# The second batch's transform input is loaded and split a step sooner, and SyncE's loads, two transpositions and token stores get a tied order

## The chip, the cores and the metric

The kernel runs on one core of one Trainium2 chip. The metric is the device time of one execution in microseconds (us). The time before is 1211.8 us, the median of three runs (1211.37, 1211.8 and 1213.98). Every time below that is not one of these comes from one profiled execution of the kernel before.

## The reference

Eight batches of 4224 tokens with 192 numbers each go through two stages. The first is a causal 7-tap convolution along the tokens, one set of softmaxed taps for each of 8 groups of 24 channels. The second adds the real part of a two-dimensional Fourier transform, normalizes each token and puts it through an MLP with a residual:

```python
out = np.einsum('hk,bskhg->bshg', w, x_unf)      # convolution, x of the rest
X = np.fft.fft(np.fft.fft(x, axis=1), axis=2)
u = x + np.real(X)
un = (u - mean(u)) / np.sqrt(var(u) + 1e-06)
result = u + np.maximum(un @ w_ch1, 0.0) @ w_ch2  # 192 -> 768 -> 192
```

## The kernel before

One token of a batch goes through these stages. Values are kept as pairs of 16-bit halves (high and low) where matmuls need the precision.

- **Convolution.** `conv_unit` (L443) multiplies windows of tokens with a band matrix on TensorE (PE) into `pc`, ScalarE (ACT) brings `pc` to `xa`, and `store_rows` (L381) writes `xa` to the scratch rows `sc` of the batch in DRAM. A batch has six chunks. For batch 1 the stores are given out by SyncE (SP), for later batches by ACT.
- **Load and split.** `load_x` (L533) reads `sc` back in another layout, in eight pieces `xs_0` to `xs_7`, given out by SP; four buffers serve the eight. `split_x` (L584) makes of each piece the halves XH on ACT (L594) and XL on VectorE (DVE, L602). Its scale `s_x` comes from the norm of the whole batch.
- **Transform.** `stage_a` (L608) multiplies XH and XL into `pa` and splits the result to `yh` (ACT) and `yl` (DVE), in 16 units per batch. `stage_b` (L660) makes `pb` and from it `V`, in 8 units. `prep` (L745) makes `pq`, adds it to the token rows `u` (DVE, L787, five instructions), takes the statistics (L794, L795 on DVE) and normalizes on GpSimd (POOL) to `hl`.
- **MLP.** `transposes` (L851) has SP give out the transposition of `hl` to `kt` (three buffers). `mlp_hidden` (L869) makes one sixth of the hidden layer: five matmuls into `ph` (L884, two PSUM buffers), `hh` on ACT (L888) and `hlo` on DVE (L889); a buffer of `ph` is free when `hlo` is done. `mlp_out` (L893) makes `po` (L903 to L909) and adds it to `u` on DVE (L915). `store_out` (L923) has SP write `u` to the output.

A batch has nine tiles of tokens, so the main loop (L1127) runs over 72 steps; step n has the hidden layer of tile n and the output layer of tile n−1. Steps 0 to 8 are those of batch 0, step 9 is the first of batch 1. Beside them, the front stages of later batches (convolution to `stage_b`) are strewn over the steps: `front` (L971) picks from tables by `rel`, the step minus the batch's first step. Batch 1 has tables of its own, `conv_1`, `load_1`, `split_1` and `a_1` (L963 to L966), since its front begins in the start-up; for it rel −9 is step 0.

Names: the profile writes `xs`, `kt` and so on without numbers. In the text `ph_3_4` is sixth 4 of step 3, `hlo_3_2` the low half of sixth 2 of step 3, `XH_1` and `XL_1` the halves made of `xs_1`, and `kt_2` the transposition for step 2 of the batch.

Each engine runs its instructions in the order in which a scheduler has put them, and a DMA is given out by the engine in whose order it stands. The scheduler goes by the order in which the program issues them and by its own costs; `tc.issue_after(x)`, also written `after(x)`, puts an instruction behind x. `in_turn()` puts XH behind the latest `hh` that was written before it. `turn[0]` is the latest transposition.

Of the kernel before, what the change touches and what calls it, by code (L numbers as in the profile page):

```python
# [35 lines left out]
AC = 32  # L36
# [93 lines left out]
def kernel(  # L130
# [250 lines left out]
    def store_rows(bt, xa, r0, cols):  # L381

        nw = xa.shape[1]
        full = min(nw, (S - r0) // WR)
        queue = nc.scalar if bt.b > 1 else nc.sync
        again = min(nw, max(0, (DUP - r0) // WR))
        for base, n in ((r0, full), (r0 + S, again)):
            if n:
                with after(turn[0] if bt.b == 1 else None):
                    store = queue.dma_start(  # L390
                        bt.sc[base : base + n * WR, cols].rearrange(
                            "(w p) d -> p w d", p=WR
                        ),
                        xa[:, :n],
                    )
        if full < nw:
            with after(turn[0] if bt.b == 1 else None):
              store = queue.dma_start(
                bt.sc[r0 + full * WR : S, cols], xa[: S % WR, full]
            )  # L400
        return store.ins
# [41 lines left out]
    def conv_unit(bt, ch, part, xa_slot=("xa", 2), slot=("f", 4), home=None):  # L443
# [41 lines left out]
        if part == 2:  # L485
            cols = slice(0, xt.shape[2])
            if b == 1:
                squares(bt, xt, bt.evicted)
            bt.last_store = store_rows(bt, xa[:, :, cols], ch * WC * WR, cols)
            del bt.xt[ch], bt.xa[ch]  # L490

    def conv_segments(bt):

# [39 lines left out]
    def load_x(bt, i):  # L533
# [5 lines left out]
        for c0, c1, wrap in ((0, cut, 0), (cut, 4, S)):  # L539
            if c0 == c1:  # L540
                continue
            src = bass.AP(
                bt.sc.tensor,
                bt.sc.offset + (33 * AC * c0 + 128 * b0 - wrap) * D,
                [[33 * D, AC * (c1 - c0)], [128 * D, b1 - b0], [1, D]],
            )
            with tc.issue_after(turn[0]) if b == 1 else ExitStack():
                load = nc.sync.dma_start(xs[AC * c0 : AC * c1, : b1 - b0], src)
        bt.xs[i] = xs
        return load.ins  # L550

    def load_first_x(bt):

# [297 lines left out]
    def transposes(bt, it):  # L851
        hl = bt.hl[it]
        n = hl.shape[1]
        kt = sb.tile([128, n, 128], F16, tag="kt", name=f"kt_{bt.b}_{it}", bufs=3)
        turn[0] = nc.sync.dma_start_transpose(kt, hl.rearrange("p n d -> p (n d)")).ins
        bt.kt[it] = kt.rearrange("p (g i) t -> p i g t", i=3)


# [63 lines left out]

    def store_out(bt, it):  # L923
        u = bt.u.pop(it)
        if it == Q0:
            nc.sync.dma_start(out0[bt.b], u[:, 0])
        else:
            nc.sync.dma_start(out1[bt.b, it].rearrange("p (g d) -> p g d", g=4), u)


    class Batch:
        def __init__(self, b):
            self.b = b
            self.nsq = 0
            self.V, self.xr, self.hl, self.kt = {}, {}, {}, {}
            self.u, self.h, self.po, self.xs, self.xt = {}, {}, {}, {}, {}
            self.xa = {}
# [13 lines left out]
    def call(f, *a):  # L951
        return lambda: f(*a)
# [8 lines left out]


    conv_1 = {-9: [4, 5]}  # L963
    load_1 = {-8: [0, 1, 2, 3], -7: [4, 5, 6, 7]}
    split_1 = {-7: [0, 1, 2, 3], -6: [4, 5, 6, 7]}
    a_1 = {-5: range(16)}  # L966

    def pause():
        pass
# [157 lines left out]
    for n in range(len(steps) + 1):  # L1127
# [24 lines left out]
                at.setdefault(min(first + i * step, len(main) - 1), []).append(f)  # L1152

        if n > 1:
            place([call(store_out, *steps[n - 2])], 0, 1)
        if n + 2 < len(steps):
            place(rest(n + 2), 0, 1)
            place([call(transposes, *steps[n + 2])], 3, 1)
        if n + 3 < len(steps):
            place(sums(n + 3), 2, 2)  # L1160
        if n + 5 < len(steps):
# [2 lines left out]
        for i, unit in enumerate(main):  # L1164
            merged += [unit, *at.get(i, ())]
        spread(merged, *fills)
    store_out(*steps[-1])


# [56 lines left out]
```

## Time and profile before

| what | value |
|---|---|
| median of three runs | 1211.8 us |
| the profiled execution's own time | 1214.54 us |
| its span, first to last instruction | 1212.7 us |
| PE busy | 1155.2 us (95%) |
| DVE busy | 891.5 us (74%) |
| POOL busy | 810.6 us (67%) |
| ACT busy | 637.2 us (53%) |
| share of PE in the chain that ended last | 86% |

The profile names the engines PE, DVE, ACT, POOL and SP; PEld is PE's load of weights, and a q behind an engine's name is the engine giving out a DMA. Times count from the start of the span. A row of the view by time tells the start, the length, the engine, the line, the operation with destination and source, how many were merged into the row, and in brackets how long the engine stood idle before and what ended that. The ends of PE's rows are modelled, so one begins before the last is listed as ended. The granted clock is 1.00 where PE runs at its full 2.4 GHz and 0.50 where it runs at 1.2.

Some starts in this execution, by the first `ph` of the step: step 1 at 115.72 us, step 2 at 129.63, step 3 at 144.64, step 4 at 162.74, step 9 at 249.06, step 10 at 268.85.

### The profile page before, as it was taken

What the parts mean: (1) busy time and instruction counts of PE and PEld (TensorE: products, weight loads), DVE (VectorE), ACT (ScalarE), POOL (GpSimd) and SP (SyncE); (2) the same over time, 40 slices, a digit from 0 to 9 for tenths busy, and PEclk for the clock granted to TensorE, in tenths of its full rate; (3) what the DMA queues carried; (4) which work ended last, traced back from release to release, by engine and by line L of the source; (5) the groups of instructions that cost most, each with busy time, mean ns of one, the idle gap of its engine ahead of it and who ended that gap; (6) DMA issues with size and microseconds to landing.
All of it is one profiled execution on the core that took longest, in us unless ns stands there. A gap on an engine that the chain in (4) does not pass through costs nothing.

```text
span 1212.7 us, 31442 instructions
## 1 busy us (share of the span) xinstructions
PE 1155.2 (95%) x12736; PEld 913.9 (75%) x12736; DVE 891.5 (74%) x2124; ACT 637.2 (53%) x1020; POOL 810.6 (67%) x1104
## 2 busy tenths in 40 slices
PE   4279999989999999999999999999999999999998
PEld 4178768867878778787877878787787878787766
DVE  7657686787867977688777978679777887566543
ACT  5547566555655556655655655555555554333222
POOL 0217875399747897389954997479963899677940
PEclk9589999989999999999999999999999999999999
DMA  8945856366565647474663956556474643333221
GB/s 307 257 119 149 219 166 147 110 170 122 150 162 141 145 122 182 133 173 115 152 170 100 200 117 175 137 146 167 114 179 124 160 104 76 89 65 92 69 56 43
DMA packets 238370, 170.56 MB, mean 141 GB/s; under 512 B 119369, under 2 KB 221969, under 8 KB 238225
## 3 DMA queue, kind: packets, MB, share of 16 engines
q1 hardware_dynamic: 184744, 109.95, 37.3%
q10 hardware_dynamic: 46952, 45.24, 13.6%
q0 software_dynamic: 6528, 13.38, 4.4%
q8 instruction: 99, 1.62, 0.6%
q14 instruction: 47, 0.38, 0.1%
HBM read 83.82 MB, written 58.55 MB: 117 GB/s over the span
## 4 chain that ended last, share of the span: by engine, by line
PE 86%; DVE 5%; DMA 4%; ACT 2%; issue 2%; SPq 1%; ACTq 0%; another core or an unknown queue 0%; DVEq 0%
PE ph L884 33%; PE po L903 10%; PE po L909 10%; PE po L906 10%; PE pa L619 6%; PE pq L769 6%; PE pb L672 5%; PE pc L468 4%; PE pa L646 1%; DMA xs<-sc 1%; PE pc L473 1%; DMA xs_yl<-sc 1%; DMA XL<-in_w_dram 1%; ACT XH L594 1%; DVE hlo L889 1%
## 5 line engine op out<-in xcount | busy, mean ns | idle before, releaser
L884 PE MATMUL ph<-kt,W 128*128 128x512 f16 (+1 forms) x2160 | 497.7, 363 | 6.4 <-DVE hlo L889 6.3
L888 ACT ACTIVATE hh<-ph 128x512 f16<-128x512 f32 (+1 forms) x400 | 236.6, 593 | 354.7 <-PE ph L884 336.8
L909 PE MATMUL po<-W,hlo 128*128 128x192 f16 x1584 | 384.5, 246 | 0.0
L903 PE MATMUL po<-W,hh 128*128 128x192 f16 x1584 | 384.4, 246 | 0.1
L906 PE MATMUL po<-W,hh 128*128 128x192 f16 x1584 | 384.1, 246 | 0.0
L889 DVE SCALAR_TENSOR_TENSOR hlo<-ph,hh 128x512 f16<-128x512 f32 (+1 forms) x400 | 269.0, 676 | 117.6 <-ACT hh L888 114.6
L884 PEld LDWEIGHTS <-W 128*128 128x128 f16 x2160 | 192.4, 98 | 142.6 <-issue 9.4
L824 POOL TENSOR_SCALAR un<-u,mv,y 128x192 f32<-128x192 f32 x260 | 274.9, 1065 | 7.8
L718 POOL DMA_INDIRECT u<-sc,rows_sb x136 | 154.5, 1136 | 31.4 <-issue 30.8
L903 PEld LDWEIGHTS <-hh 128*128 128x128 f16 x1584 | 154.8, 98 | 24.0 <-issue 0.3
L906 PEld LDWEIGHTS <-hh 128*128 128x128 f16 x1584 | 154.7, 98 | 21.4 <-issue 0.5
L909 PEld LDWEIGHTS <-hlo 128*128 128x128 f16 x1584 | 154.8, 98 | 19.7 <-issue 0.3
L841 POOL TENSOR_TENSOR hl<-un,hl 128x512 f16<-128x512 f32 (+2 forms) x142 | 129.3, 932 | 5.6
L787 DVE SCALAR_TENSOR_TENSOR u<-pq,g,u 128x128 f32<-128x128 f32 (+1 forms) x328 | 102.9, 380 | 28.5 <-PE pq L769 24.5
L815 POOL TENSOR_SCALAR v<-mv 128x4 f32<-128x4 f32 (+1 forms) x71 | 20.1, 282 | 145.7 <-DVE mv L795 128.2
L602 DVE SCALAR_TENSOR_TENSOR XL<-xs,s_x,XH 128x768 f16<-128x768 f32 (+1 forms) x56 | 93.2, 1664 | 22.9 <-ACT XH L594 22.9
L915 DVE SCALAR_TENSOR_TENSOR u<-po,fo,u 128x384 f32<-128x384 f32 (+1 forms) x136 | 81.1, 597 | 27.0 <-PE po L909 26.9
L594 ACT ACTIVATE XH<-xs,s_x 128x768 f16<-128x768 f32 (+1 forms) x56 | 94.3, 1686 | 9.1 <-DMA xs<-sc 9.0
L769 PE MATMUL pq<-c_sb,V 128*128 128x130 f16 (+1 forms) x1440 | 96.8, 215 | 0.1
L627 ACT ACTIVATE yh<-pa 99x512 f16<-99x512 f32 x112 | 65.2, 594 | 47.2 <-PE pa L619 40.3
L769 PEld LDWEIGHTS <-V 128*128 128x128 f16 (+1 forms) x1440 | 82.2, 100 | 8.3 <-issue 2.2
L619 PE MATMUL pa<-c_sb,XH 128*128 128x128 f16 x896 | 86.5, 219 | 0.0
(158 smaller groups left out, 1740.3 us busy)
## 6 DMA issues: line engine op xcount, KB each, us to landing
out_dram<-u SPq DMA_DIRECT2D x64, 384.0 KB
xt<-in_xw_dram ACTq DMA_DIRECT2D x30, 576.0 KB
sc<-xa ACTq DMA_DIRECT2D x30, 540.0 KB
xs<-sc SPq DMA_DIRECT2D x28, 288.0 KB
u<-sc SPq DMA_DIRECT2D x72, 96.0 KB
xt<-in_xw_dram SPq DMA_DIRECT2D x10, 576.0 KB
sc<-xa SPq DMA_DIRECT2D x10, 540.0 KB
xs<-sc SPq DMA_DIRECT2D x28, 192.0 KB
```

The costliest lines, as they stand in the source:

```text
L594: split = nc.scalar.activation(part(XH), src, AF.Copy, scale=bt.c)
L619: nc.tensor.matmul(pa[:, i], x[:, at], F[:, l], start=(n == 0), stop=(n == 2))
L718: nc.gpsimd.indirect_dma_start(to, None, bt.sc[:S], bass.IndirectOffsetOnAxis(ap=rows_sb[:, col : col + 1], axis=0),)
L769: mm = nc.tensor.matmul(po, weights(v, ND * r + k3), rhs[:, 0] if it == Q0 else rhs, start=(r + n == 0), stop=(r == 1 and n == 2),)
L824: (nc.vector if b + it == 0 else nc.gpsimd).tensor_scalar(un[:, g], u[:, g], mv[:, g, 0:1], y[:, g : g + 1], op0=ALU.subtract, op1=ALU.mult,)
L841: lower = (nc.vector if b + it == 0 else nc.gpsimd).tensor_tensor(bl[:, :, o : o + n], un[:, :ng, f], hi[:, :, f], op=ALU.subtract)
L884: nc.tensor.matmul(ph[:, n], W1[:, w, ht * 128 : (ht + 1) * 128], kt[:, k], start=(i == 0), stop=(i == len(order) - 1),)
L888: anchor[0] = nc.scalar.activation(hh, ph, AF.Relu).ins
L889: nc.vector.scalar_tensor_tensor(hlo, ph, 0.0, hh, op0=ALU.max, op1=ALU.subtract)
L903: nc.tensor.matmul(po[:, g % 2], hh[:, ht, tk], W2[:, ht, 0], start=(ht == 0), stop=False)
L906: nc.tensor.matmul(po[:, g % 2], hh[:, ht, tk], W2[:, ht, 1], start=False, stop=False)
L909: nc.tensor.matmul(po[:, g % 2], hlo[:, ht, tk], W2[:, ht, 0], start=False, stop=(ht == 5),)
```

## The change

Four edits. The tables of batch 1 move its loads from steps 1 and 2 to steps 0 and 1, its splits from steps 2 and 3 to steps 1 and 2, and the first eight of its sixteen `stage_a` units from step 4 to step 3. Its loads are no longer put behind the latest transposition, nor are the stores of its last two convolution chunks; the transpositions for steps 2 and 3 are put behind its last load that the program has issued by then. The store of a token tile is put behind the latest transposition, and stands in the program at the fifth place of its step where it stood at the first. In steps 0 and 1 the transposition for two steps later is issued at the end of the step.

```diff
--- before.py
+++ after.py
@@ -386,7 +386,7 @@
         again = min(nw, max(0, (DUP - r0) // WR))
         for base, n in ((r0, full), (r0 + S, again)):
             if n:
-                with after(turn[0] if bt.b == 1 else None):
+                with after(turn[0] if bt.b == 1 and not bt.ends else None):
                     store = queue.dma_start(
                         bt.sc[base : base + n * WR, cols].rearrange(
                             "(w p) d -> p w d", p=WR
@@ -394,7 +394,7 @@
                         xa[:, :n],
                     )
         if full < nw:
-            with after(turn[0] if bt.b == 1 else None):
+            with after(turn[0] if bt.b == 1 and not bt.ends else None):
               store = queue.dma_start(
                 bt.sc[r0 + full * WR : S, cols], xa[: S % WR, full]
             )
@@ -488,6 +488,7 @@
                 squares(bt, xt, bt.evicted)
             bt.last_store = store_rows(bt, xa[:, :, cols], ch * WC * WR, cols)
             del bt.xt[ch], bt.xa[ch]
+            bt.ends = ch > 2
 
     def conv_segments(bt):
 
@@ -544,10 +545,9 @@
                 bt.sc.offset + (33 * AC * c0 + 128 * b0 - wrap) * D,
                 [[33 * D, AC * (c1 - c0)], [128 * D, b1 - b0], [1, D]],
             )
-            with tc.issue_after(turn[0]) if b == 1 else ExitStack():
-                load = nc.sync.dma_start(xs[AC * c0 : AC * c1, : b1 - b0], src)
+            load = nc.sync.dma_start(xs[AC * c0 : AC * c1, : b1 - b0], src)
         bt.xs[i] = xs
-        return load.ins
+        bt.loaded = load.ins
 
     def load_first_x(bt):
 
@@ -852,7 +852,10 @@
         hl = bt.hl[it]
         n = hl.shape[1]
         kt = sb.tile([128, n, 128], F16, tag="kt", name=f"kt_{bt.b}_{it}", bufs=3)
-        turn[0] = nc.sync.dma_start_transpose(kt, hl.rearrange("p n d -> p (n d)")).ins
+        with after(batches[1].loaded if bt.b == 0 and it in (2, 3) else None):
+            turn[0] = nc.sync.dma_start_transpose(
+                kt, hl.rearrange("p n d -> p (n d)")
+            ).ins
         bt.kt[it] = kt.rearrange("p (g i) t -> p i g t", i=3)
 
 
@@ -922,16 +925,19 @@
 
     def store_out(bt, it):
         u = bt.u.pop(it)
-        if it == Q0:
-            nc.sync.dma_start(out0[bt.b], u[:, 0])
-        else:
-            nc.sync.dma_start(out1[bt.b, it].rearrange("p (g d) -> p g d", g=4), u)
+        with after(turn[0]):
+            if it == Q0:
+                nc.sync.dma_start(out0[bt.b], u[:, 0])
+            else:
+                nc.sync.dma_start(
+                    out1[bt.b, it].rearrange("p (g d) -> p g d", g=4), u
+                )
 
 
     class Batch:
         def __init__(self, b):
             self.b = b
-            self.nsq = 0
+            self.nsq, self.ends = 0, False
             self.V, self.xr, self.hl, self.kt = {}, {}, {}, {}
             self.u, self.h, self.po, self.xs, self.xt = {}, {}, {}, {}, {}
             self.xa = {}
@@ -961,9 +967,9 @@
 
 
     conv_1 = {-9: [4, 5]}
-    load_1 = {-8: [0, 1, 2, 3], -7: [4, 5, 6, 7]}
-    split_1 = {-7: [0, 1, 2, 3], -6: [4, 5, 6, 7]}
-    a_1 = {-5: range(16)}
+    load_1 = {-9: [0, 1, 2, 3], -8: [4, 5, 6, 7]}
+    split_1 = {-8: [0, 1, 2, 3], -7: [4, 5, 6, 7]}
+    a_1 = {-6: range(8), -5: range(8, 16)}
 
     def pause():
         pass
@@ -1152,10 +1158,11 @@
                 at.setdefault(min(first + i * step, len(main) - 1), []).append(f)
 
         if n > 1:
-            place([call(store_out, *steps[n - 2])], 0, 1)
+            place([call(store_out, *steps[n - 2])], 4, 1)
         if n + 2 < len(steps):
             place(rest(n + 2), 0, 1)
-            place([call(transposes, *steps[n + 2])], 3, 1)
+            if n > 1:
+                place([call(transposes, *steps[n + 2])], 3, 1)
         if n + 3 < len(steps):
             place(sums(n + 3), 2, 2)
         if n + 5 < len(steps):
@@ -1164,6 +1171,8 @@
         for i, unit in enumerate(main):
             merged += [unit, *at.get(i, ())]
         spread(merged, *fills)
+        if n < 2:
+            transposes(*steps[n + 2])
     store_out(*steps[-1])
```

What that does to the order on the engines, at three places.

The first place is in steps 0 to 2, on SP and on ACT. SP in steps 0 and 1: `sc` with `xa_5` are the last rows of batch 1, `xs` its loads, `kt` the transpositions for batch 0's steps, `u_0` the output of step 0. Before:

```order
L855 DMA_TRANSPOSE kt_2_1357<-hl_2_1299 128x12x128
L390 DMA sc_951<-xa_5_1392 120x5x192
L398 DMA sc_951<-xa_5_1392 24x192
L928 DMA out_dram<-u_0_622 128x768
L548 DMA xs_0_1543<-sc_951 128x4x192
L855 DMA_TRANSPOSE kt_3_1588<-hl_3_1529 128x12x128
L548 DMA xs_1_1599<-sc_951 128x5x192
```

Now, from the store of chunk 4 on:

```order
L390 DMA sc_951<-xa_4_1285 120x6x192
L856 DMA_TRANSPOSE kt_1_1109<-hl_1_1105 128x12x128
L390 DMA sc_951<-xa_5_1325 120x5x192
L398 DMA sc_951<-xa_5_1325 24x192
L548 DMA xs_0_1445<-sc_951 128x4x192
L548 DMA xs_1_1460<-sc_951 128x5x192
L548 DMA xs_2_1464<-sc_951 96x4x192
L548 DMA xs_2_1464<-sc_951 32x4x192
L548 DMA xs_3_1500<-sc_951 96x4x192
L548 DMA xs_3_1500<-sc_951 32x4x192
L548 DMA xs_4_1547<-sc_951 64x4x192 x2
L856 DMA_TRANSPOSE kt_2_1503<-hl_2_1304 128x12x128
```

The two stores stand ahead of kt_2 and not behind it; seven groups of loads follow them at once, with no transposition or output store between; kt_2 comes behind xs_4.

ACT in steps 1 and 2, where XH are the splits and `hh_1_2` is sixth 2 of step 1's hidden layer. Before:

```order
L231 ACTIVATE r_x_1485<-r_x_1485 128x1
L888 ACTIVATE hh_1_1495<-ph_1_2_1591 128x512
L888 ACTIVATE hh_1_1495<-ph_1_3_1628 128x512
L888 ACTIVATE hh_1_1495<-ph_1_4_1663 128x512
L681 ACTIVATE V_7_1688<-pb_7_0_1689 128x102x4
L888 ACTIVATE hh_1_1495<-ph_1_5_1680 128x512
L363 DMA xt_0_1723<-in_xw_dram 128x1152
L681 ACTIVATE V_7_1688<-pb_7_1_1704 128x102x4
L888 ACTIVATE hh_2_1725<-ph_2_0_1727 128x512
L888 ACTIVATE hh_2_1725<-ph_2_1_1771 128x512
L594 ACTIVATE XH<-xs_0_1543,s_x_1489 128x64x12
```

Now:

```order
L231 ACTIVATE r_x_1427<-r_x_1427 128x1
L681 ACTIVATE V_6_1468<-pb_6_0_1469 128x102x4
L681 ACTIVATE V_6_1468<-pb_6_1_1484 128x102x4
L594 ACTIVATE XH<-xs_0_1445,s_x_1431 128x64x12
L594 ACTIVATE XH<-xs_1_1460,s_x_1431 128x64x15
L891 ACTIVATE hh_1_1505<-ph_1_2_1604 128x512
L594 ACTIVATE XH<-xs_2_1464,s_x_1431 128x64x12
L891 ACTIVATE hh_1_1505<-ph_1_3_1644 128x512
L681 ACTIVATE V_7_1706<-pb_7_0_1707 128x102x4
L681 ACTIVATE V_7_1706<-pb_7_1_1722 128x102x4
```

XH_0 has moved from behind `hh_2_1` to the front of `hh_1_2`, with XH_1 next to it.

The second place is on DVE, at the end of step 2 and in step 3. Before, where XL_1 to XL_4 stand between the `hlo` of step 3:

```order
L889 SCALAR_TENSOR_TENSOR hlo_2_1726<-ph_2_5_1920,hh_2_1725 128x512
L602 SCALAR_TENSOR_TENSOR XL<-xs_1_1599,s_x_1489,XH 128x64x15
L889 SCALAR_TENSOR_TENSOR hlo_3_1934<-ph_3_0_1935,hh_3_1933 128x512
L415 TENSOR_SCALAR tot_0_1953<-nrm_1951 128x1
L602 SCALAR_TENSOR_TENSOR XL<-xs_2_1640,s_x_1489,XH 128x64x12
L915 SCALAR_TENSOR_TENSOR u_2_1111<-po_2_0_1967,fo,u_2_1111 128x384
L889 SCALAR_TENSOR_TENSOR hlo_3_1934<-ph_3_1_1996,hh_3_1933 128x512
L602 SCALAR_TENSOR_TENSOR XL<-xs_3_1720,s_x_1489,XH 128x64x12
L423 TENSOR_SCALAR wr_0_1957<-pn_0_1955 128x1
L602 SCALAR_TENSOR_TENSOR XL<-xs_4_1768,s_x_1489,XH 128x64x12
L787 SCALAR_TENSOR_TENSOR u_6_1533<-pq_6_2004,g_255,u_6_1533 128x192 x2
```

Now, the same stretch of `hlo`:

```order
L892 SCALAR_TENSOR_TENSOR hlo_2_1746<-ph_2_3_1878,hh_2_1745 128x512
L602 SCALAR_TENSOR_TENSOR XL<-xs_6_1656,s_x_1431,XH 128x64x12
L892 SCALAR_TENSOR_TENSOR hlo_2_1746<-ph_2_4_1912,hh_2_1745 128x512
L892 SCALAR_TENSOR_TENSOR hlo_2_1746<-ph_2_5_1929,hh_2_1745 128x512
L602 SCALAR_TENSOR_TENSOR XL<-xs_7_1738,s_x_1431,XH 128x64x12
L892 SCALAR_TENSOR_TENSOR hlo_3_1942<-ph_3_0_1943,hh_3_1941 128x512
L415 TENSOR_SCALAR tot_0_1996<-nrm_1994 128x1
L892 SCALAR_TENSOR_TENSOR hlo_3_1942<-ph_3_1_2031,hh_3_1941 128x512
```

Here the splits of xs_5 to xs_7 stand among step 2's `hlo`, and none stands behind `hlo_3_0`.

The third place is on ACT in step 7, where chunk 5 of batch 2's convolution is evicted to `xa_5` and stored. Before:

```order
L888 ACTIVATE hh_7_3340<-ph_7_2_3449 128x512
L888 ACTIVATE hh_7_3340<-ph_7_3_3486 128x512
L482 ACTIVATE xa_5_3249<-pc_5_0_3250,wg_5_3142 120x3x6x24
L482 ACTIVATE xa_5_3249<-pc_5_3_3270,wg_5_3142 120x3x6x24
L681 ACTIVATE V_2_3298<-pb_2_0_3299 128x102x4
L681 ACTIVATE V_2_3298<-pb_2_1_3314 128x102x4
L888 ACTIVATE hh_7_3340<-ph_7_4_3518 128x512
L482 ACTIVATE xa_5_3249<-pc_5_6_3330,wg_5_3142 120x2x6x24
L390 DMA sc_2047<-xa_5_3249 120x5x192
L398 DMA sc_2047<-xa_5_3249 24x192
L888 ACTIVATE hh_7_3340<-ph_7_5_3535 128x512
```

Now:

```order
L891 ACTIVATE hh_7_3340<-ph_7_0_3342 128x512
L891 ACTIVATE hh_7_3340<-ph_7_1_3380 128x512
L482 ACTIVATE xa_5_3249<-pc_5_0_3250,wg_5_3142 120x3x6x24
L482 ACTIVATE xa_5_3249<-pc_5_3_3270,wg_5_3142 120x3x6x24
L681 ACTIVATE V_2_3298<-pb_2_0_3299 128x102x4
L681 ACTIVATE V_2_3298<-pb_2_1_3314 128x102x4
L482 ACTIVATE xa_5_3249<-pc_5_6_3330,wg_5_3142 120x2x6x24
L891 ACTIVATE hh_7_3340<-ph_7_2_3448 128x512
L390 DMA sc_2101<-xa_5_3249 120x5x192
L398 DMA sc_2101<-xa_5_3249 24x192
L231 ACTIVATE r_x_3435<-r_x_3435 128x1
L891 ACTIVATE hh_7_3340<-ph_7_3_3486 128x512
```

The two stores stood behind `hh_7_4` and now stand behind `hh_7_2`.

## Rows read from the trace of the kernel before

**Rows 1.** The page, its first part (busy time of each engine, share of the span, instructions) and the first line of the chain that ended last, by engine.

```profile
PE 1155.2 (95%) x12736; PEld 913.9 (75%) x12736; DVE 891.5 (74%) x2124; ACT 637.2 (53%) x1020; POOL 810.6 (67%) x1104
...
PE 86%; DVE 5%; DMA 4%; ACT 2%; issue 2%; SPq 1%; ACTq 0%; another core or an unknown queue 0%; DVEq 0%
```

**Rows 2.** Who PE waited for from 110 us to the end of the span: engine, line and tile that waited, then what it waited for; total us, how often, the longest.

```profile
PE ph L884 <- DVE hlo L889: 6.3, 3, 3.4
PE pc L468 <- ACT xh L435: 1.9, 1, 1.9
```

**Rows 3.** Two stretches of 5 us: length, busy us of PE, PEld, DVE, ACT and POOL (each with its instructions), the granted clock, the DMA engines' share, GB/s.

```profile
155.00:160.00 5.00, 2.93 (x11) 1.51 (x11) 4.57 (x19) 0.60 (x2) 4.85 (x6) 0.71 0.48 150
255.00:260.00 5.00, 2.70 (x13) 1.30 (x13) 5.00 (x12) 0.81 (x2) 4.47 (x6) 0.61 0.65 188
```

**Rows 4.** Instructions of PE in order of time, steps 1 to 3: start, length, engine, line, operation, tile and operands, how many, and in brackets the idle time before them with what ended it. Eight `po` stand between 159.16 and 160.44, each of them in a row like the first.

```profile
115.72 1.24 PE L884 MATMUL ph<-kt,W 128*128 128x512 f16 x5
...
125.72 1.24 PE L884 MATMUL ph<-kt,W 128*128 128x512 f16 x5
...
144.64 1.24 PE L884 MATMUL ph<-kt,W 128*128 128x512 f16 x5
...
157.07 2.29 PE L884 MATMUL ph<-kt,W 128*128 128x512 f16 x5 [2.62 <-DVE hlo L889]
159.16 0.37 PE L909 MATMUL po<-W,hlo 128*128 128x192 f16 x1
...
160.44 0.29 PE L909 MATMUL po<-W,hlo 128*128 128x192 f16 x1
```

**Rows 5.** The same for PE in steps 9 and 10. The 24 `pb` matmuls run from 259.39 to 261.44.

```profile
257.30 2.29 PE L884 MATMUL ph<-kt,W 128*128 128x512 f16 x5 [3.38 <-DVE hlo L889]
259.39 0.38 PE L672 MATMUL pb<-c_sb,yh 99*128 99x102 f16 x2
...
261.44 1.97 PE L884 MATMUL ph<-kt,W 128*128 128x512 f16 x5
...
268.85 1.24 PE L884 MATMUL ph<-kt,W 128*128 128x512 f16 x5
```

**Rows 6.** Instructions of DVE in order of time, step 3.

```profile
145.92 1.90 DVE L602 SCALAR_TENSOR_TENSOR XL<-xs,s_x,XH 128x960 f16<-128x960 f32 x1 [1.17 <-ACT XH L594]
...
149.22 1.57 DVE L602 SCALAR_TENSOR_TENSOR XL<-xs,s_x,XH 128x768 f16<-128x768 f32 x1 [0.74 <-ACT XH L594]
...
151.24 0.68 DVE L889 SCALAR_TENSOR_TENSOR hlo<-ph,hh 128x512 f16<-128x512 f32 x1
151.84 1.55 DVE L602 SCALAR_TENSOR_TENSOR XL<-xs,s_x,XH 128x768 f16<-128x768 f32 x1
...
153.37 1.53 DVE L602 SCALAR_TENSOR_TENSOR XL<-xs,s_x,XH 128x768 f16<-128x768 f32 x1
154.82 1.54 DVE L787 SCALAR_TENSOR_TENSOR u<-pq,g,u 128x192 f32<-128x192 f32 x5
...
156.34 0.68 DVE L889 SCALAR_TENSOR_TENSOR hlo<-ph,hh 128x512 f16<-128x512 f32 x1
```

**Rows 7.** Instructions of ACT in order of time about the end of step 7 and in steps 8 and 9; ACTq is ACT giving out a DMA.

```profile
237.47 0.47 ACTq L398 DMA_DIRECT2D sc<-xa  x1
...
246.04 1.64 ACT L594 ACTIVATE XH<-xs,s_x 128x768 f16<-128x768 f32 x1 [2.06 <-DMA xs<-sc]
250.06 1.98 ACT L594 ACTIVATE XH<-xs,s_x 128x960 f16<-128x960 f32 x1 [2.38 <-DMA xs<-sc]
```

**Rows 8.** DMAs given out by SP in order of time: start and length of the giving out, line, destination and source. The first two are of the start of the kernel, where batch 0's rows are stored and loaded.

```profile
30.67 1.44 SPq L398 DMA_DIRECT2D sc<-xa  x1
35.60 2.13 SPq L575 DMA_DIRECT2D xs_yh<-sc  x3
...
121.45 0.83 SPq L390 DMA_DIRECT2D sc<-xa  x1
122.33 0.49 SPq L398 DMA_DIRECT2D sc<-xa  x1
...
235.33 0.35 SPq L928 DMA_DIRECT2D out_dram<-u  x1
...
239.81 1.65 SPq L855 DMA_TRANSPOSE kt<-hl  x1
241.65 3.48 SPq L548 DMA_DIRECT2D xs<-sc  x6
```

**Rows 9.** An instruction of ACT at the end of step 0: the eviction that completes the last rows of batch 1's convolution.

```profile
114.75 0.41 ACT L482 ACTIVATE xa<-pc 120x288 f32<-120x288 f32 x1 [0.23 <-PE pc L473]
```

**Rows 10.** DVE from 120 to 144 us in one stretch: length, busy time (instructions), granted clock of TensorE, the DMA engines' share, GB/s.

```profile
120.00:144.00 24.00, 16.58 (x46) 1.00 0.83 212
```

**Rows 11.** Two kinds of instruction of DVE in steps 1 and 2, as the rows of time have them.

```profile
128.24 0.57 DVE L683 SCALAR_TENSOR_TENSOR V<-pb,V 128x408 f16<-128x408 f32 x1
...
137.55 0.35 DVE L794 BATCH_NORM_STATS2 st<-u 128x6 f32<-128x192 f32 x1
```

**Rows 12.** Two more DMAs given out by SP: a store of batch 1's rows in step 0, and the transposition for step 10.

```profile
110.17 0.32 SPq L390 DMA_DIRECT2D sc<-xa  x1
...
263.66 1.52 SPq L855 DMA_TRANSPOSE kt<-hl  x1
```

**Rows 13.** ACT in step 51: the giving out of batch 7's segment stores.

```profile
926.28 3.73 ACTq L513 DMA_DIRECT2D sc<-sg  x2
```

## The prediction

> **What bounds the kernel now.** I read the page first: TensorE (PE) is busy 95% of the span and holds 86% of the chain that ended last [rows 1]. So nothing done elsewhere counts until it lets PE stand still, and the next view is who PE waited for. From 110 us to the end there are only four such waits, 8.2 us in all: three of the hidden layer's matmuls `ph` for `hlo` on VectorE (DVE), the longest 3.4 us, and one of the convolution `pc` for `xh` on ScalarE (ACT) [rows 2]. The stretches with PE below 5.00 of 5 us show where two of them lie, and that the clock falls with them: 155 to 160 us at a granted 0.71, 255 to 260 at 0.61 [rows 3]. So each costs its idle time and a tail at the lower of TensorE's two levels, 1.2 instead of 2.4 GHz.
>
> Gap A, 157.07 us: PE stood still 2.62 us. Then five `ph` took 2.29 us instead of 1.24, 1.05 lost, and eight `po` took from 159.16 to 160.44, of which half, 0.64, is lost [rows 4]. Together 4.3 us. Gap B, 257.30 us: 3.38 us idle, five `ph` again 1.05 more, the pb matmuls from 259.39 to 261.44 half lost (1.0), the next five `ph` 1.97 (0.7) [rows 4, 5]. Together 6.2 us. Gap C, 931 us: 1.9 us, with the clock staying up [rows 2].
>
> What released them is on DVE and ACT. At gap A, `ph_3_4` needs the PSUM buffer that `hlo_3_2` frees at 156.34 + 0.68. In front of that stand, with no idle time, two XL of 1.55 and 1.53 us and five L787 of 1.54 us, back to the `hlo` before at 151.24 [rows 6]: batch 1's splits, which come late in step 3. At gap B ACT waited: XH_0 of batch 2 began at 246.04 after 2.06 us for its load, XH_1 at 250.06 after 2.38, and the first `hh` of step 9 stands behind XH_1 [rows 7]. These loads were issued from 241.65, and SP, which issues in order, stood at the store of u_6 until 235.33 (it waits for DVE's `u`), and kt_0 went out at 239.81 [rows 8]. Batch 2's last convolution store was issued on ACT at 237.47, 4.2 us before the load that reads it [rows 7, 8].
>
> **The change part by part.** *The splits go a step forward (cost).* Seven XL leave steps 3 and 4, and all eight stand in steps 1 and 2, where one stood. When does the first start? The last store of batch 1's scratch rows is no longer behind kt_2: its data, `xa`, is there at 114.75 + 0.41 = 115.16 [rows 9]. Two issues of together some 1.3 us [rows 8] put its end at 116.5. From the end of such an issue to the issue of the load that reads the rows, the start of the kernel shows 30.67 + 1.44 = 32.11 to 35.60, 3.5 us [rows 8]; so xs_0 goes out at 120.0. Batch 2's xs_0 took 246.04 − 241.65 = 4.4 us from issue to XH, xs_1 250.06 − 241.65 = 8.4 [rows 7, 8]. So XH_0 begins at about 124.4, XH_1 between 126.1 and 128.4. Both stand in front of `hh_1_2` on ACT.
>
> The Trainium skill, "DMA: Bandwidth & Descriptors", section "Anatomy of one DMA", puts a fixed 2 us on each DMA, most of it the wait until the last byte is confirmed written, and HBM the slowest target. Store and load would by it take 2 us each beside their bytes; the rows' 3.5 and 4.4 us agree with that in kind, and by the page alone xs_0 would be split some 2 us sooner and the loss below smaller by as much.
>
> DVE then has, up to `hlo_1_2`: XH_1's end (127.9 to 130.4 with 1.98 us), XL_1 1.90 [rows 6, 7], 0.4 of statistics, `hlo` 0.6: 130.8 to 133.3. `ph_1_4`, which PE began at 125.72 [rows 4] and is ready for at about 128.5 now (the work now ahead of it, pq_5 and most of pb_7, stood behind it), waits for this: a new gap of 2.3 to 4.8 us, and with it the lower clock, as at gaps A and B. What decides is not this gap but DVE's queue behind it, which holds, up to `hlo_2_4` that frees the buffer for `ph_3_0`: eight `hlo` of 0.6, three u taken as long, five XL of 1.5, two V of 0.55, five L787 of 1.5 together, and four BATCH_NORM_STATS2 of 0.3 with their aggregates, 1.5 [rows 6, 11]: 6.6 + 7.5 + 1.1 + 1.5 + 1.5 = 18.2 us (durations taken a little short, since on DVE one begins some 0.08 us before the last is listed as done). `ph_3_0` starts at 149.0 to 151.5, where it started at 144.64 [rows 4]: 4.4 to 6.9 us late. The lower clock after the new gap lies inside this, since PE's own 16 us of work from `ph_1_4` to `ph_3_0` fit beside 18.2 of DVE's with 2 to spare.
> I take **+5.5**. Lower bound: DVE was busy 16.58 of the 24 us from 120 to 144 [rows 10], so 7.4 idle; what is added there, XL_1 to XL_6 at 1.90 and five times 1.55, is 9.6; even if every idle moment were used, **+2.2**. Upper: 6.9, and a second fall of the clock as after gap B, 2.8, not hidden: **+9.7**.
>
> *What that takes away at gap A (gain).* The XL in front of `hlo_3_2` are gone, 3.1 us of DVE against 2.62 of wait. Part of `pa` and its DVE half `yl` come into step 3 in exchange, but one at a time between `hlo`, where the XL stood two in a row. **−4.3**, at worst −2.6 when the wait shrinks to some tenths and the clock still falls.
>
> *SP's order.* Loads are no longer tied behind transposes, but kt_2 now stands behind xs_4, whose buffer XL_0 frees at about 127.5, and kt_3 behind xs_7, which waits for XL_3 at about 139. Five issues later kt_3 is out by 143, against `ph_3_0` at 149. Before, step 10 began at 268.85 with its kt issued from 263.66 to 265.18 and no wait of PE for it [rows 5, 12], so 3.7 us is lead enough. kt_1 stands behind a store that was issued at 110.17 [rows 12] and goes out by 112, and step 1 began at 115.72 [rows 4]. Covered: **0**; if not, rival 4 below. The stores of u come later by a step; nobody but a later load into the same buffer waits for them: **0**, and where they stop holding SP at 235.33, a gain that belongs to gap B.
>
> *Gap B (gain).* With `transposes` and stage-a units moved, the planner also spreads steps 6 and 7 anew: batch 2's last convolution store stands in front of `hh_7_3`, before it was behind `hh_7_4`. That is two sixths of the hidden layer and the `po` between them, some 5 us of PE. On SP the xs loads now stand in front of the store of u_6 and of two u loads. The load of xs_0 then needs only its rows (4.2 us after their store) and goes out about 5 us sooner than before, more than the 4.4 us that ACT lost at XH_0 and XH_1. The same order of XH and `hh` stands at the five later batch boundaries and costs PE nothing there: no further wait for `hlo` of note is in [rows 2]. I take **−5.0** of the 6.2, since DVE, full from 255 to 260 [rows 3], may leave a few tenths and a short tail; bounds 0 (rival 3) and −6.2.
>
> *Gap C.* In step 51 one `hh` stands ahead of ACT's long issue of 3.73 us [rows 13] that made `xh` late; that the row of it moves at all is by the renewed spread. **−0.5**, from 0 to −1.9.
>
> Sum: 5.5 − 4.3 − 5.0 − 0.5 = −4.3 us. The profiled execution took 1214.54 us, its span 1212.7 with 1.8 around it, and is itself 2.7 above the median of the runs, 1211.8. The sum is a difference inside the span, so it goes from the median: **1207.5 us**.
>
> **The rivals.**
> 1. *ACT becomes the bound at step 1, and the result is slower.* Seven groups of loads are given out back to back, right behind the scratch stores; xs_1 lands 8.4 us after xs_0's issue or later, `hh_1_2` is held to 131, the gap in step 1 exceeds 5 us, and the clock falls twice, in steps 1 and 2. For it: XH_1 of batch 2 did wait like that [rows 7]. Against it: the output store and the loads of u that surrounded them at 235 to 242 stand later now. Price: +9.7 there; if the later start also leaves half of gap B, 3.1, the sum is 9.7 − 4.3 − 3.1 = +2.3, and with gap A's tail kept (1.7) +4.0: about **1215.5**. It decides when XH_1 starts later than 130. In the Trainium skill the same page, section "Queues, rings and completion order", says that a DMA's completion signal comes only after every earlier write of that DMA engine; that would favour this rival, and no row here separates it.
> 2. *DVE takes the splits into its idle time.* Then +2.2, and all gaps go: 2.2 − 4.3 − 6.2 − 1.0 = −9.3: **1202.5**. For it: 7.4 us of idle. Against it: the idle time lies partly before s_x and the loads are there.
> 3. *Gap B stays, since it is DVE or POOL that set it.* DVE is busy all of 255 to 260 [rows 3]. Then 5.5 − 4.3 − 0.5 = +0.7: **1212.5**, no change. Against it: the idle time of ACT at XH_0 and XH_1, 4.4 us, is longer than the gap.
> 4. *kt_2 or kt_3 comes late* behind the loads on SP, and PE waits for a transposition in step 2 or 3. If xs_4's wait for XL_0 lasts to 131, kt_2 lands at 134 and `ph_2_0` at about 136 is still served; it takes 2 us more than that. Then some 2 us on top of the forecast: **1209.5**; a part of the forecast's own range.
>
> **How the numbers follow.** Forecast with rival 4: 0.43, own range 1204 to 1210. Rival 1: 0.17. Rival 2: 0.18. Rival 3: 0.22. A difference of 0.2%, 2.4 us, is about what a measurement of this kernel can tell from no change. Faster by more: the forecast and rival 2, less 0.02 for the forecast's upper edge: 0.59. The same: rival 3 and those 0.02: 0.24. Slower: rival 1: 0.17. The range reaches from rival 2 (1202) to just past rival 3 (1213.5) and leaves out most of rival 1 and a little below 1202.
>
> **What would show it.** In the profile of the changed kernel: a wait of `ph` for `hlo` at about 128 us, 2 to 5 us, with the granted clock below 1.00 behind it; XH_0 at 124 to 125; the first matmul of step 3 at 149 to 151; no wait in step 3; no wait in step 9, ACT's XH_0 and XH_1 of batch 2 without idle time for xs in front. I am wrong if step 3 starts before 147.5 or after 152.5, if a wait for `kt` appears, or if the gap at step 9 is still over 1 us.

## The result, and the profile after

The changed kernel took 1220.36 us (median of 6 runs, 1218.52 to 1225.57) and the kernel before, run beside it, 1213.37 us (6 runs). The ratio is 1.0066, 95% interval 1.0045 to 1.0087: slower by 0.7%, where 1207.5 was forecast and 1213.5 was the upper end. The profiled execution of the changed kernel took 1219.26 us with a span of 1217.5, 4.8 more than before.

Who PE waited for from 110 us to the end, as in [rows 2]:

```profile
PE ph L887 <- DVE hlo L892: 5.2, 3, 3.6
PE po L906 <- DVE u L918: 4.6, 4, 1.9
PE ph L887 <- DMA kt<-hl: 2.0, 1, 2.0
PE po L912 <- DVE hlo L892: 0.8, 1, 0.8
```

Four waits have become nine. `pc` no longer waits for `xh` (gap C is gone), but a wait for a transposition and four of `po` for DVE's `u` are new, and the longest wait of `ph` for `hlo` is still 3.6 us. Where they lie, by stretches of 5 us with the columns of [rows 3]:

```profile
115.00:120.00 5.00, 2.97 (x27) 2.13 (x26) 1.46 (x5) 1.87 (x5) 4.85 (x6) 1.00 0.74 169
135.00:140.00 5.00, 3.11 (x28) 2.07 (x26) 5.00 (x12) 1.10 (x2) 4.70 (x4) 1.00 0.72 206
155.00:160.00 5.00, 4.98 (x67) 4.07 (x65) 3.48 (x14) 3.29 (x5) 4.08 (x8) 1.00 0.75 192
250.00:255.00 5.00, 3.06 (x39) 2.30 (x35) 5.00 (x15) 3.21 (x5) 0.97 (x2) 1.00 0.61 143
255.00:260.00 5.00, 5.00 (x60) 3.61 (x59) 5.00 (x12) 1.88 (x4) 3.65 (x8) 1.00 1.02 241
965.00:970.00 5.00, 1.35 (x12) 0.68 (x10) 5.00 (x8) 2.78 (x4) 4.47 (x5) 0.76 0.53 136
970.00:975.00 5.00, 5.00 (x35) 3.18 (x34) 5.00 (x15) 1.62 (x3) 4.55 (x9) 0.56 0.73 146
```

Gap A is gone: 155 to 160 us has 4.98 us of PE at full clock. Gap B is a wait without a fall of the clock (250 to 260). But at 965 to 975 us, where the kernel before had no gap over 0.3 us, PE stands still and the granted clock falls to 0.56. PE by time:

```profile
118.54 1.25 PE L887 MATMUL ph<-kt,W 128*128 128x512 f16 x5 [2.03 <-DMA kt<-hl]
...
253.85 0.24 PE L906 MATMUL po<-W,hh 128*128 128x192 f16 x1 [1.94 <-DVE u L918]
...
969.15 2.29 PE L887 MATMUL ph<-kt,W 128*128 128x512 f16 x5 [3.65 <-DVE hlo L892]
```

The first is step 1, which waits 2.03 us for kt_1. The last is step 54, the first of batch 6, while batch 7 is split.

A way to see where time goes is to compare the start of each step with the kernel before. The changed kernel is 0.85 us later at step 0, 2.82 at step 1, 6.34 at step 3, 1.60 at step 9, then 2.28 us *earlier* at step 10 (as forecast, in kind), 1.28 earlier at step 19, level at step 37, 1.12 earlier at step 54 and 4.75 later from step 55 to the end. Up to step 10 the kernel did in the main what was forecast; what lost was at the batch boundaries after it, most of it in step 54.

### The profile page after: what moved, and what is told of

Read it like the earlier page. It is cut to its first block, busy times and chain, and to the rows that moved or that the text cites. A ratio compares the mean times of both kernels' runs of the same rounds, so it can differ in the third digit from the quotient of the medians.

```text
span 1217.5 us, 31495 instructions
## 1 busy us (share of the span) xinstructions
PE 1155.1 (95%) x12736; PEld 914.0 (75%) x12736; DVE 890.2 (73%) x2124; ACT 638.1 (52%) x1020; POOL 809.4 (66%) x1104
## 4 chain that ended last, share of the span: by engine, by line
PE 82%; DVE 6%; DMA 6%; issue 3%; ACT 1%; SPq 1%; POOL 1%; DVEq 0%; ACTq 0%; POOLq 0%
PE ph L887 32%; PE po L906 10%; PE po L912 10%; PE po L909 10%; PE pa L619 6%; PE pq L769 5%; PE pc L468 4%; PE pb L672 4%; DMA xs<-sc 2%; DMA sc<-xa 1%; DVE u L787 1%; DVE hlo L892 1%; PE pa L646 1%; DMA xs_yl<-sc 1%; DMA XL<-in_w_dram 1%
## 5 line engine op out<-in xcount | busy, mean ns | idle before, releaser
L824 POOL TENSOR_SCALAR un<-u,mv,y 128x192 f32<-128x192 f32 x260 | 288.6, 1116 | 7.8
L718 POOL DMA_INDIRECT u<-sc,rows_sb x136 | 162.1, 1192 | 31.5 <-issue 31.5
L815 POOL TENSOR_SCALAR v<-mv 128x4 f32<-128x4 f32 (+1 forms) x71 | 17.2, 243 | 141.9 <-DVE mv L795 136.3
```

Source lines behind the costliest of these rows:

```text
L718: nc.gpsimd.indirect_dma_start(to, None, bt.sc[:S], bass.IndirectOffsetOnAxis(ap=rows_sb[:, col : col + 1], axis=0),)
L824: (nc.vector if b + it == 0 else nc.gpsimd).tensor_scalar(un[:, g], u[:, g], mv[:, g, 0:1], y[:, g : g + 1], op0=ALU.subtract, op1=ALU.mult,)
```

## The experiments

All are the changed kernel with the edit shown, unless something else is said. Ratios are to the kernel before on the same chip; the start-up up to step 0 took 5 to 8 us less on some chips for every kernel, so times of different chips aren't compared, ratios are. Step starts are given against those of the kernel before; where a stretch from step 0 is meant, the text says so. All of them come from one execution of each kernel.

**One store and one load change places.** What stood in front of xs_1 of batch 7 in the changed kernel is SP's output store of tile 5 of batch 5 (the expectation calls it "of batch 6"; the instruction is the same). SP by time, then ACT:

```profile
955.74 0.45 SPq L932 DMA_DIRECT2D out_dram<-u  x1
956.24 2.91 SPq L548 DMA_DIRECT2D xs<-sc  x5
...
962.52 2.00 ACT L594 ACTIVATE XH<-xs,s_x 128x960 f16<-128x960 f32 x1 [4.13 <-DMA xs<-sc]
```

```diff
-        if n > 1:
+        if n > 1 and n != 52:
             place([call(store_out, *steps[n - 2])], 4, 1)
...
+        if n == 52:
+            with after(batches[7].loaded):
+                store_out(*steps[n - 2])
```

> Only edit to the changed kernel: on SP the store of u_5 of batch 6 changes places with the load of xs_1 of batch 7 that stands behind it; every other engine's order is the same. Theory S (that store, tied in front of the load, makes xs_1 late, holds ACT at XH_1 and opens the 3.65 us gap with its clock tail in step 54): XH_1 of batch 7 starts by 958 to 959 instead of 962.52, no wait of PE above 0.5 us near 969, about 6 us less than the changed kernel, near 1214.5. Theory D (xs_1 is late because the rows of batch 7 are stored 3 us later and the DMA engines are full there, whatever stands in between): XH_1 moves by under 1.5 us, the gap stays above 2 us, at most 2 us less than the changed kernel.

1216.16 us against 1212.7, ratio 1.0030 (1.0017 to 1.0044). The same rows of this kernel, where only SP's order differs in the trace, and PE's only wait there:

```profile
957.70 0.53 SPq L548 DMA_DIRECT2D xs<-sc  x1
958.33 0.46 SPq L932 DMA_DIRECT2D out_dram<-u  x1
...
962.02 1.99 ACT L594 ACTIVATE XH<-xs,s_x 128x960 f16<-128x960 f32 x1 [1.63 <-DMA xs<-sc]
...
968.23 1.24 PE L887 MATMUL ph<-kt,W 128*128 128x512 f16 x5 [0.38 <-DVE hlo L892]
```

From its issue to XH_1 the load took 962.02 − 957.70 = 4.3 us, where it took 962.52 − 956.24 = 6.3 behind the store, and the wait fell from 3.65 to 0.38 us with no fall of the clock. Step 54 now loses 1.6 us against before and not 5.9. So the place of one store on SP is worth 4 us in step 54. Theory S had 6: the last 1.6 us stay without a gap. XH_1 comes 2.8 us earlier counted from the start of step 54. It missed the "958 to 959", since this execution was 2.3 us later at step 54 than that of the changed kernel, most of it by a wait of `po` for `u` of 2.16 us in step 27, where no row of this edit stands (more on it under s_undone).

**kt_1 in front of the chunk 4 store.**

```diff
-            bt.ends = ch > 2
+            bt.ends = ch > 3
```

> Only edit to the changed kernel: on SP the transposition kt_1 of batch 0 changes places with the store of batch 1's chunk 4 in front of it, as it stood before the change. Theory Q (kt_1's packets queue behind the 540 KB of that store, its giving out took 4.41 us instead of 1.44): the wait of 2.03 us at the start of step 1 goes, step 3 starts at 149 instead of 150.98, about 2 us less than the changed kernel, near 1218.4. Theory P (kt_1 is late because POOL made hl_1 late): the wait stays within 0.5 us and the time is the same.

Ratio 1.0043 (1.0027 to 1.0060). SP of the changed kernel, and of this one:

```profile
109.64 4.40 SPq L856 DMA_TRANSPOSE kt<-hl  x1
```

```profile
107.33 1.44 SPq L856 DMA_TRANSPOSE kt<-hl  x1
108.85 6.73 SPq L390 DMA_DIRECT2D sc<-xa  x2
```

Behind the 540 KB store the giving out of the transposition takes 4.40 us, in front of it 1.44, and then PE waits for no transposition. Theory Q holds for the wait, but not for its price of 2 us. From step 0 to step 3 the changed kernel loses 5.5 us on the kernel before and this one 4.6, only 0.9 less, since in step 1 a wait of `ph` for `hlo` grows from 0.52 to 1.23 us: DVE's queue holds PE there too. The price also varies. Two other kernels below with kt_1 in front lose 4.4 and 4.6 us up to step 3 (p0_kt1, store_ahead); of those with kt_1 behind the store, three lose 4.7 to 5.4 (s_place0, s_notie, s_undone), but one_store and store_b2 7.4 and 7.5, since there the waits for kt_1, 2.30 and 2.44 us, were followed by a granted clock of 0.50. So the place of kt_1 is worth some tenths to 3 us.

**The store edit undone, and its two halves.** s_undone has neither the tie nor the fifth place; s_place0 keeps the tie, s_notie the place.

```diff
-        with after(turn[0]):
-            if it == Q0:
-                nc.sync.dma_start(out0[bt.b], u[:, 0])
...
+        if it == Q0:
+            nc.sync.dma_start(out0[bt.b], u[:, 0])
...
-            place([call(store_out, *steps[n - 2])], 4, 1)
+            place([call(store_out, *steps[n - 2])], 0, 1)
```

> The change without its store edit: output stores stand at the first place of their step and are not put behind a transposition; tables, loads, chunk stores and kt_2, kt_3 as changed. Theory S (the earlier splits cost 6 us and give back gaps A and B, and what makes the kernel slower is the tied stores): near the kernel before, 1210 to 1214, no gap in step 54, step 3 still starts 5 to 6 us later than before. Theory T (the earlier splits are the loss): 1218 to 1221.

> The change with the store tied behind the latest transposition but at the first place of its step. On SP the store in front of xs_1 of batch 7 is gone by that. Theory S: no gap in step 54, 1211 to 1215. If the tie itself costs at the other batch boundaries (po waits for DVE's u there, 1.07, 1.04 and 0.52 us in the changed kernel), 1214 to 1217.

> The changed kernel without the tie of the store, which stays at the fifth place of its step. On SP the loads xs_0 and xs_1 of batch 7 then stand behind kt_0 with no store between, and the store goes out only behind several loads. Theory S (what counts is which packets stand in front of xs_0 and xs_1): no gap in step 54, 1209 to 1214. Theory P (a store later in its step costs in itself, since u's buffer comes free later and its next loads wait): 1217 to 1221.

Ratios 0.9979 (0.9966 to 0.9991), 0.9987 (0.9976 to 0.9998) and 0.9960 (0.9945 to 0.9975): each is a little faster than the kernel before, and any one half undone is enough. PE's waits in s_undone from 105 us on:

```profile
PE ph L887 <- DMA kt<-hl: 2.2, 1, 2.2
PE pc L468 <- ACT xh L435: 1.9, 1, 1.9
PE ph L887 <- DVE hlo L892: 1.8, 3, 1.1
PE po L912 <- DVE hlo L892: 0.8, 1, 0.8
```

No `po` waits for `u` and no gap is longer than 2.2 us. Its steps agree with the changed kernel's to 0.2 us up to step 9; then it is 4.70 us earlier than before at step 10 and 5.05 at the end, against 4.75 later. The store edit costs 9.8 us, by step starts: 2.4 in step 9, 1.3 in step 18, 1.4 in step 36, 0.9 in step 45, 5.9 in step 54, and 2.0 on balance got back between steps 46 and 54, where gap C goes.

In the changed kernel the loss of a step goes with how long the load behind the store takes. At the boundaries of batches 3 to 7 SP gives out xs_0, a transposition, the store and xs_1 in the changed kernel, and in s_undone the store behind xs_1. From the issue of xs_1 to XH_1 it took 6.7, 4.9, 6.4, 6.3 and 6.3 us, in s_undone 6.0, 4.7, 4.5, 5.0 and 4.5; these loads belong to steps 18, 27, 36, 45 and 54. At step 27, with 4.9 us, the changed kernel lost nothing, but in one_store and kt1_first the same load took 7.6 and 7.3 us and step 27 lost 2.5 and 2.3. So the loss at a boundary also varies from one execution to the next.

**The store edit alone**, in the kernel before.

> The kernel before with the store edit alone (output stores at the fifth place of their step and behind the latest transposition). Theory S (late stores put 384 KB of packets in front of the loads at the batch boundaries and cost 8 to 10 us, whatever the tables say): 1217 to 1223, a gap above 3 us in step 54, gap A in step 3 unchanged. Rival I (the loss needs both edits together, by the order that the scheduler makes of them): 1211 to 1215.

Ratio 1.0088 (1.0067 to 1.0109), and in step 54 the same gap:

```profile
964.87 2.29 PE L884 MATMUL ph<-kt,W 128*128 128x512 f16 x5 [3.65 <-DVE hlo L889]
```

So the gap in step 54 is independent of the tables (theory S, not I), and steps 18, 36 and 45 lose 1.1 to 1.5 us as in the changed kernel. Gap A stays, as waits of 1.11 and 2.15 us in step 3, since this kernel has the old tables. Step 9 is not as in either kernel: gap B is gone, but PE waits 3.23 us for a transposition at the start of the step, which neither the kernel before nor the changed one does.

**The same in step 9.** In the changed kernel and in s_undone the load xs_0 of batch 2 is given out at the same time, 238.25 and 238.24, but with an output store in front in the first; XH_0 starts at 245.50 and 243.05:

```profile
237.15 0.66 SPq L932 DMA_DIRECT2D out_dram<-u  x1
238.25 3.53 SPq L548 DMA_DIRECT2D xs<-sc  x5
...
245.50 1.67 ACT L594 ACTIVATE XH<-xs,s_x 128x768 f16<-128x768 f32 x1 [2.29 <-DMA xs<-sc]
```

```profile
238.24 2.04 SPq L548 DMA_DIRECT2D xs<-sc  x4
...
243.05 1.65 ACT L594 ACTIVATE XH<-xs,s_x 128x768 f16<-128x768 f32 x1
```

The edit is that of one_store with step 7 and `batches[2]`.

> Only edit to the changed kernel: on SP the output store of u_5 of batch 0 goes from in front of the loads xs_0 and xs_1 of batch 2 to behind them, and one part of xs_3 moves up by it; every other engine's order is the same. Theory Q (XH_0 of batch 2 begins 2.45 us later in the changed kernel than in s_undone, 245.50 against 243.05, with the load given out at the same 238.25, since the store's packets stand in front): XH_0 at 243, the wait of po for DVE's u of 1.94 us in step 9 goes, about 2 us less than the changed kernel's ratio, 1.005. Rival (the wait comes from DVE's own queue): XH_0 moves, the wait stays above 1.5 us, ratio 1.0066.

Ratio 1.0043 (1.0027 to 1.0060). SP and ACT of this kernel:

```profile
233.01 0.94 SPq L548 DMA_DIRECT2D xs<-sc  x2
234.12 0.40 SPq L932 DMA_DIRECT2D out_dram<-u  x1
...
237.54 1.64 ACT L594 ACTIVATE XH<-xs,s_x 128x768 f16<-128x768 f32 x1
```

From the issue of the load to XH_0 it is 237.54 − 233.01 = 4.5 us, and there is no wait of PE from 235 to 262 us. From step 9 to step 10 it gains 6.3 us on the kernel before, as s_undone does; the changed kernel gained 3.9. Theory Q again. The ratio's interval overlaps that of the changed kernel; it is the step starts that show the gain.

**The converse: a store put in front of that load.** First p0_kt1, the fast kernel for it (place 0, tie kept, kt_1 first):

> The change with the output store at the first place of its step (tie kept) and with kt_1 in front of the chunk 4 store. The two gains of the runs so far, 9.7 and 1.4 to 3 us off the changed kernel, add if they are independent: 1208 to 1210. If kt_1's wait was only cover for the splits in step 1 (DVE bound), 1210.5 as with the first alone.

Ratio 0.9949 (0.9932 to 0.9966), without a wait for a transposition. That is below s_place0 alone (0.9987, 0.9976 to 0.9998), from which only kt_1 differs, so by the ratios the two gains add. They were taken on different chips, though, and the two profiled executions differ by only 0.8 us from step 0 to the end; s_place0's waited 1.0 us for kt_1. Then, with p0_kt1, the load of xs_1 of batch 7 is written behind the store of step 51 and tied to it:

```diff
-        loads = [call(load_x, bt, ch) for ch in load.get(rel, ())]
+        loads = [
+            call(load_x, bt, ch) for ch in load.get(rel, ())
+            if (bt.b, ch) != (7, 1)
+        ]
...
+                if n == 53:
+                    with tc.issue_after(out_put):
+                        load_x(batches[7], 1)
```

> The converse of one_store, in the fast kernel p0_kt1: on SP the output store of u_6 that stands behind the load xs_1 of batch 7 is put in front of it; no other engine's order changes. In p0_kt1 xs_1 took 4.46 us from its issue to XH_1. Theory Q (packets of the store stand in front of the load's): 6.2 to 6.7 us from issue to XH_1, as in the kernels with the store in front. Theory two (the gap of step 54 needs this and the convolution's last store 3 us later, which this kernel doesn't have): XH_1 some 2.5 us later, wait of PE there under 1 us, time as p0_kt1, ratio 0.995. Theory one (the store alone makes the gap): gap above 2.5 us, about 5 us more, ratio 0.999.

Ratio 0.9964 (0.9952 to 0.9977). SP, ACT and PE of this kernel:

```profile
946.41 0.56 SPq L932 DMA_DIRECT2D out_dram<-u  x1
947.07 3.02 SPq L548 DMA_DIRECT2D xs<-sc  x5
...
952.46 2.00 ACT L594 ACTIVATE XH<-xs,s_x 128x960 f16<-128x960 f32 x1 [2.45 <-DMA xs<-sc]
...
957.62 0.24 PE L906 MATMUL po<-W,hh 128*128 128x192 f16 x1 [1.58 <-DVE u L918]
```

The same load in p0_kt1:

```profile
940.91 0.52 SPq L548 DMA_DIRECT2D xs<-sc  x1
941.60 0.43 SPq L932 DMA_DIRECT2D out_dram<-u  x1
...
945.37 2.00 ACT L594 ACTIVATE XH<-xs,s_x 128x960 f16<-128x960 f32 x1 [0.77 <-DMA xs<-sc]
```

The load takes 5.4 us from its issue behind the store, 0.9 more than the 4.5 of p0_kt1 and less than the 6.2 that theory Q gave. Step 54 loses 1.8 us on the kernel before, and by step 63 it is 2.2, with one wait of `po` of 1.58 us and no fall of the clock. This is between the two theories: the store alone costs about 2 us, and the gap with the clock's fall seems to need a second delay. A candidate is in the order too: with the store at the fifth place, the last convolution store of batch 7 is given out 2.9 us later than before, and xs_0 with it 3.15 us later, 952.50 for 949.35. First the kernel before, then the changed one:

```profile
946.24 0.46 ACTq L398 DMA_DIRECT2D sc<-xa  x1
```

```profile
949.13 0.47 ACTq L398 DMA_DIRECT2D sc<-xa  x1
```

Steps 51 to 53 are also 2.6 us shorter there, where gap C goes. So this store goes out 11.5 us ahead of step 54 in the six kernels with the output stores at the fifth place and the tables as changed or before, and 15.6 us ahead in all kernels with them at the first place. In one_store and s_notie it is late in this way without the output store in front of xs_1, and step 54 loses 1.6 and 1.7 us. The output store alone loses 1.8, both together 5.9, neither (s_undone, p0_kt1) nothing. No run moves the convolution store by itself, so it is not shown that it is the second delay.

**Spreading the splits.** As p0_kt1, and

```diff
-    split_1 = {-8: [0, 1, 2, 3], -7: [4, 5, 6, 7]}
-    a_1 = {-6: range(8), -5: range(8, 16)}
+    split_1 = {-8: [0, 1], -7: [2, 3, 4, 5], -6: [6, 7]}
+    a_1 = {-5: range(16)}
```

> As p0_kt1, and the splits of batch 1 are strewn over three steps (2 in step 1, 4 in step 2, 2 in step 3) instead of two (4 and 4), with all stage_a units in step 4. Theory D (DVE's work in steps 1 and 2 is what costs about 4 us there): two XL less before step 3 starts, 3 us less in steps 1 and 2, no new gap in step 3: 1205 to 1208. Rival: the XL in step 3 open gap A again: 1209 to 1213.

Ratio 0.9952 (0.9935 to 0.9970), the same as p0_kt1 within the intervals. From step 0 to step 3 it loses 2.3 us on the kernel before, where p0_kt1 loses 4.4, and gap A doesn't come back (longest wait of `ph` for `hlo` in the run 0.7 us); over the profiled span that makes 0.4 us. DVE's part in steps 1 and 2 is as theory D says; what it is worth to the whole kernel can't be told from nothing.

**All together, a miss.** The tables of sp_a, kt_1 first, and the store at the fifth place without the tie (s_notie); the second with the splits as 2, 3 and 3.

> The three gains together: output stores at the fifth place but not tied (as s_notie, which also has no wait of pc for xh in step 51), kt_1 in front of the chunk 4 store, splits over three steps as sp_a. If they add: s_notie 0.996, less 1.5 us for kt_1 and 2 us for the splits: ratio 0.993. If boundaries change with each new order by as much: 0.995 to 0.997.

> As best_n with the splits as 2, 3 and 3. If DVE's work in step 2 still bounds: 1 us less than best_n. If step 3 has no room for a third XL: gap A comes back in part, 1 to 3 us more.

Ratios 0.9985 (0.9977 to 0.9994) and 0.9996 (0.9988 to 1.0005): worse than s_notie alone (0.9960), on another chip. Counted from its step 0, best_n is 5.8 us ahead of the kernel before at step 10, and loses 4.2 of it again from step 19 to step 43. That lies in four steps: 23, 27, 32 and 41 are 0.7, 1.8, 0.9 and 1.2 us longer than in s_notie. In step 27 `po` waits 1.34 us for `u`; in the other three PE stands still for 0.4 to 0.9 us, and the profile names nothing that it waited for. What caused it stays open.

## Why the prediction was wrong

*Steps 1 and 2, +5.5.* Right in mechanism; that the size came out exactly was luck in part. SP and then ACT and DVE:

```profile
116.36 1.80 SPq L398 DMA_DIRECT2D sc<-xa  x1
120.00 9.99 SPq L548 DMA_DIRECT2D xs<-sc  x8
...
123.83 1.66 ACT L594 ACTIVATE XH<-xs,s_x 128x768 f16<-128x768 f32 x1 [0.22 <-DMA xs<-sc]
125.67 2.05 ACT L594 ACTIVATE XH<-xs,s_x 128x960 f16<-128x960 f32 x1 [0.18 <-DMA xs<-sc]
127.59 0.61 ACT L891 ACTIVATE hh<-ph 128x512 f16<-128x512 f32 x1
...
130.80 0.66 DVE L892 SCALAR_TENSOR_TENSOR hlo<-ph,hh 128x512 f16<-128x512 f32 x1
```

xs_0 went out at 120.00, as worked out, but by two errors that cancel: the store's issue ended at 118.16 and not 116.5, and the load followed 1.84 us behind it and not 3.5. The end of the issue is a poor mark: from it to the load the twelve kernels with the loads moved have 1.8 to 3.1 us, from its start always 3.5 to 3.7. The 2 us for one DMA in the Trainium skill ("DMA: Bandwidth & Descriptors", section "Anatomy of one DMA") are given there for the SWDGE (gpsimd) path, which the prediction left out; these DMAs are given out by SP, and no run here shows what part of the 3.5 us such a cost has. XH_0 came at 123.83 (124.4), XH_1 at 125.67 (126.1 to 128.4), `hlo_1_2` at 130.80, `ph_3_0` at 150.98 (149.0 to 151.5). But of the 6.34 us, 0.85 are of the start-up, and of the 5.5 from step 0 about 0.9 are kt_1's: with kt_1 in front the splits cost 4.4 to 4.6. The new gap of 2.3 to 4.8 us with a fall of the clock didn't come. PE waited three times 0.5 to 1.1 us at a granted 1.00 (two of them in 135 to 140 above); that kt_1 made PE late is not the reason, since with kt_1 on time the longest is 1.24 us (p0_kt1), still at 1.00.

*Gap A, −4.3.* Right: no wait in step 3, and steps 3 to 8 together gain 4.7 us.

*SP's order, "covered: 0".* Wrong for kt_1. The step took its issue time for its arrival: it was given out from 109.64, before the 112 worked out, but behind a store of 540 KB, and took 4.40 us for it. PE waited 2.03 us, of which about 0.9 are left at step 3. A wait for a transposition was one of the prediction's own signs of being wrong.

*Gap B, −5.0.* Right for the tables: s_undone gains 6.3 us from step 9 to step 10. In the changed kernel 2.4 of it are lost to the store in front of xs_0, and the wait of 1.94 us there is another of the prediction's signs of being wrong.

*The output stores, "0".* The step that failed, and the sign with it. "Nobody but a later load into the same buffer waits for them" looked at who waits for the store's end. What it passed over is what the store stands in front of: on SP the loads of the next batch come right after the transposition to which the store was tied, at every batch boundary and not only at that of batch 1. That the order of the two is what counts is shown by one_store and store_b2; that the load's packets wait behind the store's on the DMA engines is the reading of it, not itself shown. All of the comparison of order was of steps 0 to 9; step 54 was taken to be as before. With 9.8 us for this term, 0.85 for the start-up, 5.5 for steps 0 to 2 (kt_1 in it), and −4.7 and −6.3 for the gaps, the sum is +5.2, where the profiled spans differ by 4.8. (Gap C is in the 9.8.) The forecast of −4.3 with 9.8 in place of the 0 would have been +5.5, and the medians differ by 7.0.

The rivals: none was this. Rival 1 had the sign, but its place (XH_1 in step 1) was as forecast; rival 4 had the mechanism of kt_1, for kt_2 and kt_3, and 2 us. (Rival 1's +4.0 on 1211.8 is 1215.8, and not 1215.5.)

## What to carry to other kernels

A store that nobody waits for still has a place in a queue: before moving one, look at which loads come right behind it, in every repetition of the loop, and what the reader of those loads holds up. A store of 384 KB in front of an urgent load of 384 or 480 KB cost 0.9 to 2.4 us at most boundaries here, and 4 us in step 54, where the load was late for another reason too and the clock fell. When a change has one part with a mechanism and one that "only ties the order", run each alone: here the first was worth −0.2% and the second +0.9%.

## What the runs showed of the hardware

SP was held for 4.40 us by the giving out of one transposition right behind a 540 KB store, three times the 1.44 us in front of it; over all runs it was 3.65 to 4.51 us in six kernels with the transposition behind the store and 1.44 or 1.45 in the eight others. Of the waits of PE in the kernel before and the changed one, those of 2.03 and 1.94 us left the granted clock at 1.00; those of 2.62 [rows 4], 3.38 [rows 5] and 3.65 us were followed by stretches at the lower level. The length alone doesn't tell which: a wait of 2.18 us in s_undone left the clock at 1.00, and one of 2.15 us in s_only, 3.6 us after one of 1.11, was followed by a fall.
